# Issuing the small q loads from GpSimd in place of the sync engine, in a fused attention and feed-forward kernel

## The chip, the cores and the metric

The kernel runs on one core of a Trainium2 chip. The metric is the device time of one launch in microseconds (us). Before the change the median of three runs was 926.68 us (926.6 to 928.33). The profiled execution has a span of 926.5 us, at a granted TensorE clock of 1.00.

A core has TensorE (matmul), VectorE, ScalarE and GpSimd, which compute; the sync engine, which only issues transfers; and 16 DMA engines, which carry them. In the profile these are PE (PEld is TensorE's weight load), DVE, ACT, POOL and SP. A name with q behind it, such as SPq, is the engine's instruction queue, which issues transfers and waits for semaphores.

## The reference

```python
q, k, v: (8 batches, 8 heads, 576 rows, 64)      # float32
kv  = einsum('bhsd,bhse->bhde', k, v)            # 64 x 64 per head, no softmax
out = einsum('bhsd,bhde->bhse', q, kv)
out = out / sqrt(mean(out*out, axis=-1) + 1e-6) * g_norm
x   = out.transpose(0, 2, 1, 3).reshape(4608, 512)
h   = x @ w_in                                   # w_in: 512 x 2048
g   = h * erf(softplus(h))
return g @ w_out                                 # w_out: 2048 x 512, result 4608 x 512
```

Linear attention with a normalization per row and head gives x; a feed-forward block with an unusual gate follows.

## The kernel before

**Groups.** The 4608 rows of x are cut into nine groups (`NG`) of 512 rows. Group T takes the first 512 rows of batch T; the ninth gathers the last 64 rows of all eight batches. For a group, the attention is made for four pairs of heads (`NP`), one after the other, while the feed-forward block of the group before is running. So a pair of group T+1 is a guest in the work on group T.

**Stages.** The weights come in as 64-bit words and are turned into float32 on ScalarE and VectorE (`load_w`, `w_split`, `w_join`) while group 0 is computed with plain float32 matmuls. From group 1 on (`T == FIRST - 1`) the work moves to faster products with float32r: every weight block is cut into three parts (`w_upper` on ScalarE, L596; `w_lower` on VectorE, L599 and L602), the parts are written to device memory (stores at L668 and L672), and from group 2 on they are fetched again for each group (`load_parts`, L773). A product (L634) is eight matmuls into `n_ps` and four into `m_ps`. From group 2 on the work goes in batches of four of the sixteen column blocks of w_in (`BATCH`); one batch takes about 24 us, and one pair of heads is a guest in each.

**Loads of a pair.** `load_pair(i)` fetches k and v of pair i with transfers of 288 KB or 287.5 + 0.5 KB (L141, L146). In group 0, q comes in whole (L132) and TensorE turns it. From group 1 on, `load_q` fetches q so that VectorE can turn it with one instruction per pair (L318, the transpose of 32 x 32 blocks): it needs each 32-column piece of a head in a place of its own. So q of a pair is taken in eight transfers of 32 or 40 KB, whose contiguous runs have 32 numbers, 128 bytes (L162).

**Order and queues.** The order of all instructions is written by hand; each engine's queue runs in program order and waits in order. Nearly all transfers are issued by the sync engine: q, k, v, the raw weights, the stores of cut weights, the fetches of weight parts and the results. A transfer that waits, for instance for a free buffer, holds back everything behind it on that queue. The tiles of q have two buffers (`kvp`, `bufs=2`), those of pairs 2 and 3 excepted. From group 1 on, pair i+2 is loaded in the step `loads`, next to the work on pair i; its q takes the buffer that the transpose of pair i has freed. GpSimd issues the two loads of `g_norm` at the start and sets up some constants; nothing stands on its queue afterwards.

**The deferral.** For the first two pairs of group 1 (pairs 4 and 5), `load_pair(..., turned=False)` brings only k and v. Their q is put later into the sync queue by hand: `load_q(NP)` after all raw weight loads of the opening (L758), and `load_q(NP + 1)` in the second step of group 0 (L906).

Of the kernel before, what the change touches and what calls it, by code (L numbers as in the profile page):

```python
# [61 lines left out]
def kernel(  # L62
# [10 lines left out]
    nc = tc.nc  # L73
# [6 lines left out]
    NP = H // 2  # L80
# [38 lines left out]
    def chunks(T):  # L119

        return 6 if T == 0 else 5

    def load_pair(i, turned=True):
        T, p = divmod(i, NP)
        if T >= B:
            return
        pool = early if i in (2, 3) else kvp
        side = nc.scalar if i < 3 else nc.sync
        if T == 0:
            t = pool.tile([P, G if pool is early else S], FP32, name="q_sb", tag="q")  # L130
            t = q_sb[T, p] = t[:, 0:G].rearrange("p (j h d) -> p j h d", j=J, h=2)
            nc.sync.dma_start(  # L132
                out=t, in_=q[T, 2 * p : 2 * p + 2, 0:G, :].rearrange("h (p j) d -> p j h d", j=J)
            )
        for name, got, src in (("k", k_sb, k), ("v", v_sb, v)):
            C = chunks(T)
            rows, rest = divmod(S, C)
            assert rest < 2
            t = got[T, p] = pool.tile([rows + rest, 2, C, D], FP32, name=f"{name}_sb", tag=name)
            heads = src[T, 2 * p : 2 * p + 2]  # L140
            side.dma_start(  # L141
                out=t[:rows].rearrange("r h c d -> r h (c d)"),
                in_=heads[:, : S - rest].rearrange("h (r c) d -> r h (c d)", c=C),
            )
            if rest:
                side.dma_start(  # L146
                    out=t[rows:, :, 0], in_=heads[:, S - rest :].rearrange("h r d -> r h d")
                )
        if T > 0 and turned:
            load_q(i)  # L150

    def load_q(i):


        T, p = divmod(i, NP)
        t = q_sb[T, p] = kvp.tile([P, S], FP32, name="q_sb", tag="q")
        for n in range(P // SQ):
            h, w = divmod(n, D // SQ)
            to = t[n * SQ : n * SQ + SQ].rearrange("a (j b) -> a j b", b=SQ)
            for head, js in ((1 - h, slice(0, G // 2 // SQ)), (h, slice(G // 2 // SQ, S // SQ))):  # L160
                src = q[T, 2 * p + head, :, w * SQ : w * SQ + SQ]
                nc.sync.dma_start(  # L162
                    out=to[:, js], in_=src.rearrange("(j a) b -> a j b", a=SQ)[:, js]
                )

# [108 lines left out]
    def w_next(what):  # L274
        i = w_at[what]
        if i < len(w_order):
            w_at[what] = i + 1
            {"load": load_w, "split": w_split, "join": w_join}[what](*w_order[i][1:])
# [465 lines left out]
    for i in range(NP + 3):  # L744
        for piece, p in ((0, i), (1, i - 1), (4, i - 3), (3, i - 2)):
            if 0 <= p < NP:
                first[p][piece]()
        if i == 1:
            for _ in range(RAW - 2):
                w_next("load")  # L750
            load_pair(NP, turned=False)
            load_pair(NP + 1, turned=False)
        for what in w_rounds.get(i, ()):
            w_next(what)


    w_late.append(True)
    load_q(NP)  # L758
    first_batch, batches = FIRST * NB, NG * NB
    w_seq = {  # L760
        which: [(which, f) for _ in range(NG - FIRST) for f in range(FC)] for which in ("in", "out")
# [60 lines left out]
    for n in range(FIRST * FC + 1):  # L822
        T, f = divmod(n, FC)
        if n == FC:
            early_room.close()
            late = ctx.enter_context(tc.tile_pool(name="late", bufs=1))
            x_new = ctx.enter_context(tc.tile_pool(name="x_new", bufs=1))
            acc = ctx.enter_context(tc.tile_pool(name="acc", bufs=1))
            w_in_p = ctx.enter_context(tc.tile_pool(name="w_in_p", bufs=BATCH))
            low = low_room.enter_context(tc.tile_pool(name="low", bufs=1))  # L830
            forms = late.tile([P, 3, KC, G], FP32R, name="x_forms0")
            x_forms[FIRST] = [forms[:, i] for i in range(3)]
        if T < FIRST:
            if f == 0:
                steps = pieces_of(T + 1)

            if due(0 if n == 2 * (BATCH - 1) else 1):
                weights()
            while kept:
                keep_prepared()  # L840
            for piece in steps[f][3]:
                piece()
            for key in list(w_new)[:2]:
                w_lower(*key)
            for piece in steps[f][0]:
                piece()
        while due(0):
            weights()
        done = n - LAG + 1
        if T == 0 and done >= 0:  # L850
            gates(done)
        if T == FIRST - 1:
            if f == 0:
                x_high = wide.tile([P, KC, G], FP32R, name="x_high", tag="a")
                x_low = low.tile([P, KC, G], FP32R, name="x_low")
                for i in range(0, KC, 2):
                    upper(xT[T][:, i : i + 2], x_high[:, i : i + 2])
                for i in range(0, KC, 2):
                    lower_only(xT[T][:, i : i + 2], x_high[:, i : i + 2], x_low[:, i : i + 2])
        if T == FIRST - 1 and f >= WHOLE:  # L860
            n_ps, m_ps = hidden(T, f, turns=False)
        elif T < FIRST:

            if n > 1:
                plain[n] = ps_h.tile([P, G], FP32, name="h_ps", tag="h")
                blocks = [(n, c) for c in range(KC)]
            elif n == 0:
                for i, (pool, tag) in enumerate(((ps_at, "at"), (ps_o, "o0"))):
                    plain[i] = pool.tile([P, G], FP32, name="h_ps", tag=tag)
                blocks = [(i, c) for c in range(KC - 1) for i in range(2)] + [(0, KC - 1)]  # L870
            else:
                blocks = [(1, KC - 1)]
            for i, c in blocks:
                nc.tensor.matmul(  # L874
                    plain[i],
                    lhsT=w_in_sb[:, i % FC, c],
                    rhs=xT[T][:, c, :],
                    start=(c == 0),
                    stop=(c == KC - 1),
                )  # L880
        if T < FIRST:
            if n == whole:
                old_h = acc.tile([P, BATCH, G], FP32, name="h", tag="e")
            h = hs[n] = old_h[:, n - whole] if n >= whole else unit("h_sb")
            s = ss[n] = unit("s_sb")
            if n in plain:
                nc.scalar.copy(h, plain.pop(n))
            else:
                nc.scalar.activation(h, n_ps, AF.Copy, scale=SHIFT - 1.0)
                add(h, m_ps)  # L890
            if T == FIRST - 1:
                if f == 1:
                    x_both = wide.tile([P, KC, G], FP32R, name="x_both", tag="b")
                    for i in range(0, KC, 2):
                        both_only(x_high[:, i : i + 2], x_low[:, i : i + 2], x_both[:, i : i + 2])
                    x_forms[T] = x_high, x_low, x_both
                gates(done)
                for key in list(w_new):
                    w_lower(*key)
                for key in to_cut[f]:  # L900
                    w_upper(*key)
            nc.scalar.activation(s, h, AF.Softplus)
            if n == 0:
                w_next("split")
            if n == 1:
                load_q(NP + 1)  # L906
            for piece in steps[f][1]:
                piece()
            if f % BATCH == BATCH - 1:
                for i in range(n - BATCH + 1, n + 1):  # L910
                    nc.scalar.activation(ss[i], ss[i], AF.Erf)  # L911
                softplus_table()
            if T == FIRST - 1:
                load_parts("in", {FC - 3: 2, FC - 2: 1, FC - 1: 1}.get(f, 0))
        if n >= LAG:
            T2, f2 = divmod(n - LAG, FC)
            last = n - LAG in (FC - 1, whole - 1)
            project(f2, hs[n - LAG], last)
            if last:
                sums(*((acc, "e") if T2 < FIRST - 1 else (wide, "a")))  # L920
                if T2 == 0:
                    for j in range(J):
                        store(T2, j, es.pop(j))
        if T < FIRST:
            for piece in steps[f][2]:
                piece()
# [49 lines left out]
    for m in range(first_batch, batches + 1):  # L976
        T, b = divmod(m, NB)
# [133 lines left out]
```

## Time and profile before

| Item | Value |
|---|---|
| median time | 926.68 us |
| TensorE busy | 898.8 us, 97% of the span |
| VectorE, ScalarE, GpSimd busy | 751.0, 589.9, 2.4 us |
| bytes moved by DMA | 259.91 MB in 143,210 packets |
| packets under 512 bytes | 78,936 |
| sync engine's queue of transfers (q1) | 141,432 packets, 256.74 MB, 75.7% of 16 engines |
| GpSimd's queue of transfers (q0) | 64 packets |
| q transfers from the sync engine after group 0 | 224 (112 of 40 KB, 112 of 32 KB) |

The busy time of TensorE is modelled, since matmuls overlap, and TensorE at 97% is not TensorE at its peak. The share of a DMA queue is the time that its packets took, out of 16 engines' span. An instruction that issues a transfer is not counted as busy; its duration on the queue is the time until the queue can go on. A wait is put down to the semaphore that came last.

### The profile page before, as it was taken

How to read it: one execution, taken by the hardware profiler on the slowest of the kernel's cores; microseconds unless marked ns; L12 is line 12 of the kernel's file. 1: busy time of each engine (PE TensorE's matmuls, PEld its weight loads, DVE VectorE, ACT ScalarE, POOL GpSimd, SP SyncE). 2: the span in 40 equal slices, each digit the busy share in tenths (PEclk: the TensorE clock that was granted, in tenths of full speed). 3: DMA queues.
4: the chain of work that ended last, by engine and by line, in shares of the span. 5: the costliest groups of instructions: out<-in, count | busy, mean ns of one | idle time of the engine just before them, and what ended most of it. 6: DMA issues, size and time to landing. Idle time of an engine off the chain costs nothing.

```text
span 926.5 us, 13591 instructions
## 1 busy us (share of the span) xinstructions
PE 898.8 (97%) x4990; PEld 668.6 (72%) x4990; DVE 751.0 (81%) x1088; ACT 589.9 (64%) x783; POOL 2.4 (0%) x10
## 2 busy tenths in 40 slices
PE   6999999988999999999999999999999999999998
PEld 4444445655587888778878888788878888888886
DVE  2799958888588888888888888888888888886777
ACT  3868766767675666656665666666666766665552
POOL 1000000000000000000000000000000000000000
PEclk9999999999999999999999999999999999999999
DMA  9767506698688888988898788887889788778871
GB/s 250 237 190 265 167 1 249 246 378 313 239 287 312 311 312 310 347 308 308 308 337 309 296 310 310 301 306 284 292 313 404 272 286 322 291 288 314 325 271 51
DMA packets 143210, 259.91 MB, mean 281 GB/s; under 512 B 78936, under 2 KB 101800, under 8 KB 143144
## 3 DMA queue, kind: packets, MB, share of 16 engines
q1 hardware_dynamic: 141432, 256.74, 75.7%
q10 hardware_dynamic: 1648, 2.29, 0.9%
q8 instruction: 40, 0.66, 0.3%
q14 instruction: 26, 0.21, 0.1%
q0 software_dynamic: 64, 0.00, 0.0%
HBM read 224.40 MB, written 34.60 MB: 280 GB/s over the span
## 4 chain that ended last, share of the span: by engine, by line
PE 76%; DMA 11%; DVE 6%; ACT 5%; issue 1%; SPq 1%; DVEq 0%; ACTq 0%
PE n_ps L634 41%; PE m_ps L634 20%; PE o_ps L690 6%; PE h_ps L874 4%; DMA w_out_parts<-w_out 4%; DMA w_in_parts<-w_in 2%; DMA w_in<-w_new 2%; DMA v_sb<-in_v_dram 1%; PE at_ps L449 1%; PE at_ps L435 1%; DMA w_raw<-in_moe_w_out_dram 1%; ACT s_sb L911 1%; DMA q_sb<-in_q_dram 1%; DVE h L612 1%; PE at_ps L496 1%
## 5 line engine op out<-in xcount | busy, mean ns | idle before, releaser
L634 PE MATMUL n_ps<-w_out_parts,g_forms 128*128 128x512 f32 x928 | 231.2, 391 | 1.7 <-DMA w_out_parts<-w_out 1.7
L634 PE MATMUL n_ps<-x_forms,w_in_parts 128*128 128x512 f32 x896 | 225.1, 393 | 3.2 <-DMA w_in_parts<-w_in 2.1
L634 PEld LDWEIGHTS n_ps<-w_out_parts,g_forms 128*128 128x128 f32 x928 | 172.4, 188 | 38.4 <-DMA w_out_parts<-w_out 3.3
L634 PEld LDWEIGHTS n_ps<-x_forms,w_in_parts 128*128 128x128 f32 x896 | 166.1, 188 | 41.1 <-ACT h L1024 3.2
L1039 ACT ACTIVATE s<-h 128x512 f32<-128x512 f32 x112 | 71.0, 634 | 180.9 <-DVE h L612 180.9
L612 DVE TENSOR_TENSOR h<-m_ps,h 128x512 f32<-128x512 f32 x116 | 79.9, 689 | 61.5 <-ACT h L1024 39.9
L634 PE MATMUL m_ps<-w_out_parts,g_forms 128*128 128x512 f32 (+1 forms) x468 | 124.3, 388 | 0.0
L634 PE MATMUL m_ps<-x_forms,w_in_parts 128*128 128x512 f32 x448 | 119.8, 389 | 0.0
L690 PE MATMUL o_ps<-w_out_sb,h_sb 128*128 128x512 f32 x224 | 101.5, 596 | 0.2 <-DVE h_sb L820 0.2
L634 PEld LDWEIGHTS m_ps<-w_out_parts,g_forms 128*128 128x128 f32 x468 | 87.5, 188 | 18.4
L634 PEld LDWEIGHTS m_ps<-x_forms,w_in_parts 128*128 128x128 f32 x448 | 84.1, 188 | 17.6
L612 DVE TENSOR_TENSOR e<-m_ps,e 128x512 f32<-128x512 f32 (+1 forms) x117 | 80.3, 687 | 14.1 <-PE m_ps L634 2.9
L1024 ACT ACTIVATE h<-n_ps 128x512 f32<-128x512 f32 x112 | 65.6, 585 | 16.6 <-PE n_ps L634 16.6
L690 PEld LDWEIGHTS o_ps<-w_out_sb,h_sb 128*128 128x128 f32 x224 | 41.3, 189 | 45.3 <-issue 42.8
L578 DVE SCALAR_TENSOR_TENSOR g_forms<-g_forms 128x1024 fp32r<-128x1024 f32 x58 | 71.1, 1225 | 2.0
L575 DVE TENSOR_TENSOR g_forms<-h,g_forms 128x1024 fp32r<-128x1024 f32 x58 | 70.6, 1217 | 1.2 <-ACT g_forms L572 1.1
L572 ACT ACTIVATE g_forms<-h 128x1024 fp32r<-128x1024 f32 x58 | 58.7, 1051 | 14.8 <-PE m_ps L634 10.9
L1071 DVE TENSOR_TENSOR h<-h,s 128x1024 f32<-128x1024 f32 x56 | 65.9, 1218 | 0.0
L874 PE MATMUL h_ps<-xT,w_in_sb 128*128 128x512 f32 x144 | 64.6, 594 | 0.0
L607 DVE SCALAR_TENSOR_TENSOR e<-n_ps,e 128x512 f32<-128x512 f32 x88 | 60.1, 683 | 1.5 <-PE n_ps L634 1.5
L109 ACT ACT_TABLE_LOAD x44 | 56.5, 1283 | 0.8
L874 PEld LDWEIGHTS h_ps<-xT,w_in_sb 128*128 128x128 f32 x144 | 27.1, 190 | 33.4 <-issue 31.6
(119 smaller groups left out, 990.7 us busy)
## 6 DMA issues: line engine op xcount, KB each, us to landing
w_out_parts<-w_out SPq DMA_DIRECT2D x116, 768.0 KB
w_in_parts<-w_in SPq DMA_DIRECT2D x112, 768.0 KB
w_in<-w_new SPq DMA_DIRECT2D x16, 768.0 KB
w_raw<-in_moe_w_in_dram SPq DMA_DIRECT2D x16, 512.0 KB
w_raw<-in_moe_w_out_dram SPq DMA_DIRECT2D x8, 1024.0 KB
out_dram<-e SPq DMA_DIRECT2D x32, 256.0 KB
k_sb<-in_k_dram SPq DMA_DIRECT2D x28, 287.5 KB
v_sb<-in_v_dram SPq DMA_DIRECT2D x28, 287.5 KB
```

Source lines behind the costliest of these rows:

```text
L109: nc.scalar.preload_act_table_set("softplus")
L572: nc.scalar.activation(high, x, AF.Copy, scale=1.0 + 2.0**-13)
L575: nc.vector.tensor_tensor(out=low, in0=x, in1=high.bitcast(FP32), op=ALU.subtract)
L578: nc.vector.scalar_tensor_tensor(out=both, in0=low.bitcast(FP32), scalar=SHIFT, in1=high.bitcast(FP32), op0=ALU.mult, op1=ALU.add,)
L607: nc.vector.scalar_tensor_tensor(out=out_, in0=ps, scalar=scale, in1=out_, op0=ALU.mult, op1=ALU.add)
L612: nc.vector.tensor_tensor(out=out_, in0=ps, in1=out_, op=ALU.add)
L634: nc.tensor.matmul(ps[:, cols], lhsT=weights(form, k), rhs=moving(form, k)[:, cols], start=(form == forms[0] and k == 0), stop=(form == fo ...
L690: nc.tensor.matmul(o_ps[j], lhsT=g[:, j * P : j * P + P], rhs=w_out_sb[:, f, :], start=(f == 0), stop=last,)
L874: nc.tensor.matmul(plain[i], lhsT=w_in_sb[:, i % FC, c], rhs=xT[T][:, c, :], start=(c == 0), stop=(c == KC - 1),)
L1024: nc.scalar.activation(h[:, i], n_ps, AF.Copy, scale=SHIFT - 1.0)
L1039: nc.scalar.activation(s[:, i], h[:, i], AF.Softplus)
L1071: nc.vector.tensor_tensor(out=part(h, half), in0=part(h, half), in1=part(s, half), op=ALU.mult)
```

## The change

From group 1 on, the eight transfers of q per pair are issued by GpSimd, whose queue is empty by then, and no longer by the sync engine. The runs, the buffers and the bytes are the same. With q on a queue of its own, the deferral is taken out as well: `load_pair` issues q of pairs 4 and 5 with their k and v, and the two separate calls of `load_q` go. The purpose is to keep the many small issues out of the queue that carries the weights.

```diff
-    def load_pair(i, turned=True):
+    def load_pair(i):
...
-        if T > 0 and turned:
+        if T > 0:
             load_q(i)
...
                 src = q[T, 2 * p + head, :, w * SQ : w * SQ + SQ]
-                nc.sync.dma_start(
+                nc.gpsimd.dma_start(
                     out=to[:, js], in_=src.rearrange("(j a) b -> a j b", a=SQ)[:, js]
                 )
...
-            load_pair(NP, turned=False)
-            load_pair(NP + 1, turned=False)
+            load_pair(NP)
+            load_pair(NP + 1)
...
     w_late.append(True)
-    load_q(NP)
...
-            if n == 1:
-                load_q(NP + 1)
```

## The prediction, made before the changed kernel was run

> **What bounds the kernel now.** I first read the page: busy shares, then the slices.
>
> ```profile
> PE 898.8 (97%) x4990; PEld 668.6 (72%) x4990; DVE 751.0 (81%) x1088; ACT 589.9 (64%) x783; POOL 2.4 (0%) x10
> ...
> DMA  9767506698688888988898788887889788778871
> ```
>
> TensorE is the bound, GpSimd is empty, and the DMA engines are some 80% busy without being full. Only TensorE's 27.7 us of idle time (926.5 - 898.8) can be won, and only where it goes back to the sync queue. A table by stretch places it: 8.6 us in the first 24 us, 2.6 in 24 to 48, 3.4 in 192 to 216, 2.8 in 216 to 240, 4.1 spread over 336 to 720, and 4.0 at the very end. The list of waits names the ends of these:
>
> ```profile
> DVE qT L318 <- DMA q_sb<-in_q_dram: 3.9, 1, 3.9
> PE n_ps L634 <- DMA w_in_parts<-w_in: 2.1, 2, 1.7
> PE at_ps L435 <- DVE qT L318: 2.0, 1, 2.0
> PE n_ps L634 <- DMA w_out_parts<-w_out: 1.7, 2, 0.9
> ```
>
> Columns: total us, times, longest. The two waits on weight parts (2.1 + 1.7 = 3.8 us) are nearly all of the 4.1 us. Then the sync queue's timeline before the longest:
>
> ```profile
> 581.89 7.43 SPq L162 DMA_DIRECT2D q_sb<-in_q_dram  x8
> 589.37 0.46 SPq L773 DMA_DIRECT2D w_out_parts<-w_out  x1
> 589.92 0.38 SPq L773 DMA_DIRECT2D w_in_parts<-w_in  x1
> 590.34 0.43 SPq L773 DMA_DIRECT2D w_out_parts<-w_out  x1
> 590.87 0.75 SPq L773 DMA_DIRECT2D w_in_parts<-w_in  x1
> ```
>
> Eight q transfers keep the sync queue for 7.43 us; then weight loads go out one after the other without a wait, so their buffers had been free and the loads were late only because q stood in front. In the chain, the last of these (issued 590.87) lands 10.12 us later and TensorE waits 1.7 us for it. The other three stalls show the same picture: q blocks of 7.83, 10.71 and 11.30 us end at 369.9, 466.5 and 661.3, and weights issued some us later arrive 0.8, 0.9 and 0.4 us late. While q is issued from 581 to 590 the DMA share is 0.55, against 0.82 around it: the queue is short of issue, not of bandwidth.
>
> Stage two (144 to 250 us) shows the same for stores:
>
> ```profile
> 177.41 7.30 SPq L162 DMA_DIRECT2D q_sb<-in_q_dram  x8
> 184.82 0.39 SPq L672 DMA_DIRECT2D w_out<-w_new  x1
> ...
> 188.13 0.63 ACT L596 ACTIVATE w_new<-w_out_sb 128x512 fp32r<-128x512 f32 x1 [1.44 <-DMA w_out<-w_new]
> 190.12 0.63 ACT L596 ACTIVATE w_new<-w_in_sb 128x512 fp32r<-128x512 f32 x1 [1.36 <-DMA w_in<-w_new]
> ...
> 197.25 0.49 PE L634 MATMUL n_ps<-x_high,w_new 128*128 128x512 f32 x1 [3.42 <-ACT h_sb L889]
> ```
>
> q delays the store of a cut weight, the store frees its buffer late, ScalarE waits 2.8 us, and TensorE waits for ScalarE.
>
> **What the Trainium skill says.** "DMA: Bandwidth & Descriptors", section "Issuing engines are not separate DMA queues": all issuers feed the same 16 engines, and another issuer saves only the sequencer's issue time. The issue time is just what is short here. Its section "SWDGE vs HWDGE vs iDMA" says that GpSimd's cores compute each descriptor in software, and that each DMA engine goes round its queues in turn. This trace has only two GpSimd transfers:
>
> ```profile
> L174 POOL DMA_DIRECT2D g_col<-in_g_norm_dram x2: 531/618/704, 1.2 to 1.9; - x2
> ```
>
> Each has 64 runs of one number, so this is a weak gauge. "SBUF — State Buffer", section "Who interferes with whom": VectorE's copies and tensor_scalar in a two-port mode and GpSimd exclude each other. The trace has such candidates: the CAST at L480 takes 426 ns for 512 columns, where L481 takes 692.
>
> **The change part by part.**
>
> Sync queue, removed: 28 pairs x 8 issues. A block lasts about 7.4 us without back pressure and up to 14.77 us for two pairs at the start; 28 x 7.5 = 210 us of the queue's time go. Its other work moves up only where it was ready.
> - Steady stage: the late weights were 0.4 to 1.7 us late after q blocks of at least 7.4 us. Even with q's data still sharing the engines, they come in time. Gain 3.8 us.
> - Stage two: ScalarE's 1.44 + 1.36 us before the erf batch vanish, as the stores can go about 5 us earlier. TensorE's stall of 3.42 us shrinks by 2.8. The stall at 227 us stays: there ScalarE's last wait before the erf batch is for TensorE itself (1.31 us at 220.0), so its DMA wait of 2.15 us at 218.05 gains nothing. Gain 2.8 us.
> - Start: q of the first pair of group two is issued at 36.51, behind weights, and lands at 47.64. VectorE waits 3.9 us, TensorE 2.0. From GpSimd it starts when TensorE has turned pair 0 (9.9 us) and lands by about 31 us. Gain 2.0 us.
>
> GpSimd, added: 224 transfers. A pair is 576 rows x 2 heads x 2 halves = 2304 runs of 128 bytes, 256 or 320 per transfer. Unknown: the cost of a descriptor. Lower bound, all of the 0.62 us is fixed: 5 us per pair. Upper bound, all of it is per descriptor: 0.62/64 x 2304 = 22.3 us. I take 1.5 us a transfer, 12 us per pair. Nothing else is queued on GpSimd, the transposes of successive pairs (L318) are 24.2 us apart, and a q buffer freed by one transpose is read two transposes, 48 us, later. Even 22.3 us is hidden. Cost 0.
>
> DMA engines: the q runs are small. After q has ended, 768 to 816 us, 310 GB/s take a share of 0.79: 48 x 16 x 0.79 / 14.88 MB = 40.8 engine-us per MB. Queue 1 in all: 0.757 x 16 x 926.5 = 11,222 engine-us against 256.74 x 40.8 = 10,475. The 747 over, shared by 64,512 q packets, are 11.6 ns each on top of 5.2 for the bytes: 16.8 ns, or 2.4 us of all engines per pair. Unchanged if software descriptors are as cheap. To fill the 18% left free in a period of 24.2 us (4.4 us), a packet would have to cost (4.4 + 2.4) x 16 / 2304 = 47 ns.
>
> VectorE lock: the next pair's CAST and small copies come 20 us after the transpose that releases q, so 12 us of descriptor writing misses them. In stages one and two, tensor_scalar (L250, L253) can collide, but from 50 to 190 us TensorE has no idle time at all, so what feeds it has slack, and VectorE is idle 11 us in 120 to 144. Bound 0 to 3 us; I take 0.
>
> Start, moved: the deferral goes too, so q of pairs 4 and 5 competes from 10 us on with k and v of pair 3 (issued 11.2 and 14.1, read at 20.29 without a wait) at a DMA share of 0.91. Bound: 0 if there is slack, 4.8 us if both pairs (2 x 2.4) go first. GpSimd's pace lets about one through, half of it into slack: 1.2 us lost.
>
> Sum: 926.7 - 3.8 - 2.8 - 2.0 + 1.2 = 919.3 us.
>
> **The rivals.**
> - Larger gain: no loss at the start, and earlier stores and weights also take in 4 us of what is not counted above, ScalarE's other waits on stores (9.3 - 2.8 = 6.5 us) and TensorE's weight loads on the DMA (3.3): 926.7 - 8.6 - 4 = 914 us. Against it: most of these waits lie beside others.
> - A wash: the start loses 4.8 us and VectorE's lock 3, so 926.7 - 8.6 + 7.8 = 926 us. For it: the share of 0.91 there.
> - Slower, the packets: a software-made q packet costs 60 ns. Then q takes 8.6 us of all engines per pair, the need exceeds the period by 8.6 - 2.4 - 4.4 = 1.8 us, and over some 15 steady pairs less the 4.8 us of gains at the start and in stage two: 926.7 + 27 - 4.8 = 949 us; half of it if prefetched weights cushion it, 935. Against it: no view of before shows such a price.
> - Slower, the generator: 3.5 us per transfer make 28 us per pair, 4 us over the period, over 24 pairs near 1010 us. The gauge above (at most 2.8 us for an average transfer) speaks against it.
>
> **How the numbers follow.** Forecast (gain of 4 to 10 us) 60%, larger gain 8%, wash 13%, packets 13%, generator 6%. Predicted 919.3. The range from 914.5 to 935 leaves out the generator, the worse packets and the largest gain. Faster 0.68, same 0.12, slower 0.20.
>
> **What would show it.** Right: no wait of TensorE for weight parts; the transpose L318 at about 44 us without a DMA wait; ScalarE's waits for stores shorter between 184 and 192; GpSimd's eight issues inside 24 us per pair. Wrong: a wait of L318 for q in every pair (generator), a DMA share near 1.0 with new weight stalls (packets), TensorE waiting for k or v at 20 us (start), longer CASTs (lock). The prediction falls with the descriptor's price above all.

## The result: 936.6 us, 1.2% slower

The changed kernel took 936.59 us (median of four, 935.79 to 941.56), the kernel before beside it 926.64 us (925.43 to 928.33). The ratio is 1.0117, 95% interval 1.0078 to 1.0156. The forecast was 919.3 us, faster; the time lies just outside the range.

Busy time and DMA slices of the changed kernel, from the page:

```profile
PE 904.2 (97%) x4990; PEld 668.4 (71%) x4990; DVE 752.0 (80%) x1088; ACT 589.6 (63%) x783; POOL 135.5 (14%) x234
...
DMA  9867406888799898889797889888797788778871
```

GpSimd now has 135.5 us of work, of which the issues of q are 133.1 (on GpSimd the page counts them as busy). The matmuls are the same 4990; TensorE's busy time is 5.4 us longer, but the ends of matmuls are modelled, so nothing is read into it. TensorE's waits for weight parts became (total us, times, longest)

```profile
PE n_ps L634 <- DMA w_in_parts<-w_in: 10.7, 14, 2.5
PEld n_ps L634 <- DMA w_out_parts<-w_out: 6.1, 9, 1.2
PE n_ps L634 <- DMA w_out_parts<-w_out: 2.4, 4, 0.8
```

The two PE lines were 3.8 us together; they are 13.1 us, and come 18 times, not four. (The middle line, of TensorE's weight load, was 3.3 us, five times.) The changed kernel was not behind everywhere. At 144 us the two were level; in stage two the changed kernel won, and at 244 us it was 4.0 us ahead. The matmul that had waited 3.42 us at 197.25 waits 0.87, and the second stall of that stage, at 227.12, has shrunk too (its line before, then both after):

```profile
227.12 0.50 PE L634 MATMUL n_ps<-x_high,w_new 128*128 128x512 f32 x1 [2.79 <-ACT h L889]
...
194.78 0.50 PE L634 MATMUL n_ps<-x_high,w_new 128*128 128x512 f32 x1 [0.87 <-ACT h_sb L888]
223.09 0.50 PE L634 MATMUL n_ps<-x_high,w_new 128*128 128x512 f32 x1 [1.21 <-ACT h L888]
```

From 244 us to the end it lost 12.8 us: TensorE's idle time from 288 to 720 us is 432 - 186.32 - 232.10 = 13.6 us where it was 4.1. So the loss is in the steady stage, where the forecast had put its largest gain.

GpSimd's transfers, from the view of the tile q_sb, and the two queues of the page:

```profile
L162 POOL DMA_DIRECT2D q_sb<-in_q_dram x224: 584/601/1128, 9.9 to 662.4; - x112
DMA to landing us min/median/max: 1.9/5.7/10.0
```

```profile
q1 hardware_dynamic: 73336, 248.47, 73.1%
q0 software_dynamic: 7232, 8.27, 3.8%
```

An issue takes 601 ns in the median, eight of them under 5 us a pair. The 64,512 packets of 128 bytes have become 3,584 of 2,048 or 2,560 bytes; q takes 3.8% of 16 engines, 569 engine-us, or 8.8 ns per run. Neither the making of the transfers on GpSimd nor their packets are dear.

Now the sync queue around one pair, start and duration, changed kernel first:

```profile
500.89 0.29 SPq L141 DMA_DIRECT2D k_sb<-in_k_dram  x1
...
504.55 1.13 SPq L141 DMA_DIRECT2D v_sb<-in_v_dram  x1
506.38 0.56 SPq L146 DMA_DIRECT2D v_sb<-in_v_dram  x1
508.38 6.54 SPq L772 DMA_DIRECT2D w_out_parts<-w_out  x1
515.01 0.37 SPq L772 DMA_DIRECT2D w_in_parts<-w_in  x1
```

```profile
503.81 0.56 SPq L146 DMA_DIRECT2D v_sb<-in_v_dram  x1
505.68 11.26 SPq L162 DMA_DIRECT2D q_sb<-in_q_dram  x8
516.99 0.45 SPq L773 DMA_DIRECT2D w_out_parts<-w_out  x1
517.55 0.37 SPq L773 DMA_DIRECT2D w_in_parts<-w_in  x1
```

The second fence is the kernel before. Without q, the first weight load behind k and v is itself held for 6.54 us. The queue is through with it at 514.92; before, it was through with q at 516.94. Taking q off freed 2 us, not 11: so it was not q alone that had held the q issues. The packets of the trace show what else the engines were doing. Mean number of packets in flight by kind, in steps of 2 us:

```
             before                      after
us       weights  k,v    q        weights  k,v    q
506-508    16.2   0.0  0.0            6.3  2.3  0.0
508-510    12.1   0.5  0.0            1.2  4.2  0.6
510-512     0.7   4.9  2.3            1.0  3.7  3.1
512-514     0.0   5.3  2.4            1.0  0.4  4.4
514-516     0.0   2.0  5.5            2.6  0.1  0.8
516-518     0.0   0.0  4.0           14.2  0.9  0.2
518-520    12.9   0.0  0.0           15.2  1.1  0.0
520-522    15.9   0.0  0.0           15.2  1.1  0.0
```

With weights 16 packets are in flight, with k and v five. The cause is the shape: from group 1 on k and v come as 115 rows of five, and 115 = 5 x 23. The Trainium skill, "DMA: Bandwidth & Descriptors", section "Why a DMA increments its semaphore by 16 and not by 1", says that a transfer runs on the largest number of engines up to 16 that divides the slowest dimension of both sides. For 115 that is five; the trace agrees with 4.9 to 5.3 in flight. So it was in the forecast's stretch with a DMA share of 0.55: from 584 to 586 us 5.3 k or v packets, 1.7 of q and 0.2 of weights were in flight. What the forecast read as a queue short of issue was five engines at work on k and v, and the other eleven with only some small q packets.

An estimate of what these five carry per batch, from median packet times: weights 64 x 234 ns = 15.0 us, k and v 92 x 55 = 5.1, q 144 x 12.5 = 1.8, results 8 x 84 = 0.7: 22.6 us in a period of some 24. The other eleven carry 17.5. The mean share of 0.82 hid this. After the change, q takes 8 packets of 138 ns in the mean of the two sizes, 1.1 us in place of 1.8, so by the same estimate the five carry 21.9 us: the loss isn't that they have more to carry.

And one thing differs after: from 508 to 512 one weight packet is in flight while some four k or v packets are, and from 516 to 522 some fifteen weights and one k or v. From 508.30 to 515.70 us the 22 weight packets follow one another, each starting within about 0.1 us of the end of the one before, and from 515.80 to 522.73 so do 92 k and v packets, just one engine's share of a pair. So one of the five engines still carried weights while its four fellows did k and v, and did its k and v while all others carried weights. A weight load spread over all 16 engines isn't complete before this one has carried its part. Before, q in the middle let all come out level: of the k and v packets between 300 and 660 us, a share of .007 started while 12 or more weight packets were in flight; after, .229. I call this the overlap share.

### The profile page after: what moved, and what is told of

Read it like the earlier page. It is cut to its first block, busy times and chain, and to the rows that moved or that the text cites. A ratio compares the mean times of both kernels' runs of the same rounds, so it can differ in the third digit from the quotient of the medians.

```text
span 935.3 us, 13621 instructions
## 1 busy us (share of the span) xinstructions
PE 904.2 (97%) x4990; PEld 668.4 (71%) x4990; DVE 752.0 (80%) x1088; ACT 589.6 (63%) x783; POOL 135.5 (14%) x234
## 4 chain that ended last, share of the span: by engine, by line
PE 57%; DMA 29%; DVE 6%; ACT 5%; issue 2%; SPq 0%; DVEq 0%; ACTq 0%
PE n_ps L634 29%; PE m_ps L634 14%; DMA w_out_parts<-w_out 14%; DMA w_in_parts<-w_in 8%; PE h_ps L873 6%; PE o_ps L690 5%; DMA k_sb<-in_k_dram 4%; DMA w_in<-w_new 2%; DMA q_last<-in_q_dram 1%; DVE w_new L599 1%; DMA q_sb<-in_q_dram 1%; PE at_ps L449 1%; ACT s_sb L908 1%; DVE h L612 1%; PE at_ps L435 1%
## 5 line engine op out<-in xcount | busy, mean ns | idle before, releaser
L162 POOL DMA_DIRECT2D q_sb<-in_q_dram x224 | 133.1, 602 | 522.7 <-DVE qT L318 514.9
```

The lines of the kernel that those rows point to most:

```text
L162: nc.gpsimd.dma_start(out=to[:, js], in_=src.rearrange("(j a) b -> a j b", a=SQ)[:, js])
```

## The experiments

**Theory:** k and v on five engines, nearly full, are the limit; weights directly behind k and v let one of them fall behind. **Rivals:** GpSimd's packets among the weights; the deferral; the one-row transfers. (That GpSimd issues q too late is out already: after, L318 never waits for q.) Each ratio is to the kernel before, run on the same chip in turn.

**1 and 2. Even engines.** k and v as 128 rows of four and 64 of one (both multiples of 16), once on the changed kernel, once on the kernel before. It also saves 112 small matmuls in all (4878 for 4990); the trace shows 38 of their kind in 0.75 us, so that they are worth some 2 us at most.

```diff
+            if T > 0:
+                rows, rest, C = P, R, J
...
-                out=t[:rows].rearrange("r h c d -> r h (c d)"),
+                out=t[:, :, 0:C].rearrange("r h c d -> r h (c d)"),
...
-                    out=t[rows:, :, 0], in_=heads[:, S - rest :].rearrange("h r d -> r h d")
+                    out=t[:rest, :, C], in_=heads[:, S - rest :].rearrange("h r d -> r h d")
```

> The changed kernel, with k and v of groups 1 to 7 fetched as 128 rows of 4 x 64 plus 64 rows of 64 in place of 115 rows of 5 x 64 plus one row (18 small matmuls a pair in place of 20). Theory A (uneven engines: k and v of 115 rows are carried by five of the sixteen DMA engines, one of the five falls behind once q no longer stands between k, v and the weights, and each weight load ends with it): the waits for weight parts vanish, about 916 to 921 us, and no slower than the kernel before with the same edit. Theory B (the GpSimd queue itself slows the weight loads, whatever k and v do): weight waits stay, 928 to 936 us, and clearly slower than the kernel before with the same edit.

> The kernel before (q on the sync engine, deferral kept) with the same even split of k and v. Theory A: its four stalls for weights behind q shrink too, since the q issues are no longer held up by five full engines: 918 to 924 us, near a_even. Theory B: 918 to 924 us as well, but a_even 1% above it.

Measured: 919.55 us, ratio 0.9915 (0.9901 to 0.9928), and 919.18 us, ratio 0.9911 (0.9897 to 0.9924). TensorE waits for no weight part in either. The stretch from 480 to 528 us of the changed kernel and then of its even version (TensorE, its weight load, VectorE, ScalarE, GpSimd, clock, DMA share, GB/s):

```profile
480.00:528.00 48.00, 45.42 (x275) 36.11 (x278) 40.31 (x59) 28.91 (x37) 9.36 (x16) 1.00 0.84 296
```

```profile
480.00:528.00 48.00, 47.40 (x296) 38.56 (x295) 40.85 (x61) 30.08 (x41) 8.87 (x17) 1.00 0.92 330
```

In this stretch the share and the rate rise, since k and v no longer leave eleven engines idle; from 300 to 660 us the difference is smaller (0.85 to 0.87, 302 to 307 GB/s). The sync queue of the even version waits for TensorE to free buffers for 367.6 us, where that of the changed kernel did for 199.2, so it is further ahead:

```profile
SPq L773 <- PE m_ps L635: 367.6, 109, 11.4
```

With even engines the two kernels differ by 0.4 us, so it makes no difference who issues q. That the change loses needs the uneven load.

**3. Another issuer than GpSimd:** ScalarE, `nc.scalar.dma_start` at L162.

> The changed kernel with q's eight issues on ScalarE's queue in place of GpSimd's: again a queue of its own, but with descriptors made in hardware. Theory A: one engine falls behind just the same, weight waits of 10 us or more, and ScalarE loses issue time besides: 935 to 950 us. Theory B (software descriptors are what hurts): no weight waits beyond those of before, 920 to 930 us, unless ScalarE's own issue time shows as waits of TensorE for ScalarE.

Measured: 1124.35 us, ratio 1.2107 (1.2078 to 1.2137). ScalarE's own instructions stand behind its issues, and TensorE behind these:

```profile
ACT h L1021 <- DMA q_sb<-in_q_dram: 147.5, 16, 12.2
PE n_ps L634 <- ACT h L1021: 96.6, 18, 8.4
```

Both expectations miss by far: the kernel is so much slower (DMA share 0.70 from 300 to 660 us, granted clock 0.922 over the span) that weights are never short, and for its question the run says nothing. It shows that issues can hold up a computing engine for 12 us.

**4. GpSimd alone, deferral kept** (the kernel before with `nc.gpsimd` at L162).

> The kernel before with GpSimd as issuer and the deferral kept: the change without its second part. Theories A and B: the loss lies in the steady stage, so 934 to 938 us, like the changed kernel. Theory C (the loss comes from q of pairs 4 and 5 competing at the start): near 925 us.

Measured: 937.56 us, ratio 1.0111 (1.0089 to 1.0133), overlap share .327. The issuer alone makes the whole loss.

**5. The deferral alone** (the changed kernel with `nc.sync` at L162).

> The changed kernel with the sync engine as issuer again: the second part of the change alone (q of pairs 4 and 5 asked for early, no deferral). All theories put the loss in the steady stage, so this gives 924 to 932 us; theory C (the loss comes from the start) would give 936.

Measured: 932.62 us, ratio 1.0036 (1.0021 to 1.0051), overlap share .007. This is just above the expectation. Dropping the deferral costs something with the sync engine as issuer, but does not add to the loss with GpSimd (1.0111 without, 1.0117 with it).

**6. Weights directly behind k and v, without GpSimd:** in the kernel before, `load_q(i)` stands ahead of k and v from pair 6 on.

> The kernel before, q still on the sync engine with hardware descriptors, but from pair 6 on the eight q transfers are issued ahead of the pair's k and v in place of behind them, so that weights follow directly on k and v. Theory A (what hurts is that nothing stands between the uneven k, v and the weights): one engine falls behind as in the changed kernel, waits for weight parts of 8 us or more, 932 to 940 us, with GpSimd out of the picture. Theory B (GpSimd's queue is needed for the loss): 924 to 929 us.

Measured: 951.31 us, ratio 1.0240 (1.0202 to 1.0278), overlap share .089, slower than either expectation.

```profile
PE n_ps L634 <- DMA w_in_parts<-w_in: 17.7, 20, 1.9
```

The order loses without any q transfer of GpSimd, but by a different route: q's issues hold the queue for 12 to 14 us there, and all five engines come late to the weights, not one. So the run shows a loss without GpSimd, and doesn't test the single late engine.

**7. A brake in place of q:** in the changed kernel, a store of 256 bytes of the v tile on the sync queue behind each pair's k and v from pair 8 on. The store must wait for v, so the weights do too.

```diff
+        if T > 1:
+            nc.sync.dma_start(out=dram.tile([1, D], FP32, name=f"brake{i}"), in_=t[0:1, 0, 0])
         if T > 0:
             load_q(i)
```

> The changed kernel with one more transfer on the sync queue behind each pair's k and v from pair 8 on: 256 bytes of the v tile to a scratch in device memory. It makes the sync queue wait until v has landed on all five engines before weights go out. Theory A: the lagging engine is waited for once per pair, so it cannot stay behind; the share of k and v packets that run beside weights on twelve or more engines falls from 24% to some 2%, and the time to 922 to 929 us. Theory B: weights go out later still and the slow queue stays, 937 us or more.

Measured: 927.37 us, ratio 0.9992 (0.9974 to 1.0009), overlap share .007.

```profile
PE n_ps L636 <- DMA w_in_parts<-w_in: 3.0, 1, 3.0
```

GpSimd issues the same 224 transfers, and the 13.1 us of TensorE's waits for weight parts shrink to one of 3.0. So the loss comes with the missing step between k, v and weights. The time doesn't reach the forecast 919; by the sum above (software q at 1.1 us in place of 1.8) the five engines still carry 21.9 us per batch.

**8. Without the one-row transfers** of k and v (L146), from group 1 on. The last row of each head's k and v is left out in these groups.

> The changed kernel without the one-row transfers of k and v from group 1 on; it leaves out the last row of every head's k and v in those groups. The five-engine loads of 115 rows stay. Theory A: the load on five engines is what counts, so still 932 to 938 us with weight waits. Rival: the one-row transfers, which held the sync queue for up to 4.6 us, were what the even split really removed; then 918 to 924 us.

Measured: 938.56 us, ratio 1.0100 (1.0060 to 1.0141), overlap share .283. The one-row transfers do not make the late engine late.

**9. GpSimd's packets added, q left where it was:** the kernel before plus 208 GpSimd transfers of 288 runs of 128 bytes into a spare tile that nothing reads, eight behind each transpose (L318).

> The kernel before, with its q loads left on the sync queue, plus eight further GpSimd transfers per pair (288 runs of 128 bytes each, 2304 per pair as q has) into a spare tile that nothing reads, released by the transpose as q's are in the changed kernel. It adds work and leaves out none. If order is the cause (q no longer stands between k, v and the weights): the DMA engines stay in step, the share of k and v packets that run beside weights on 12 or more engines stays under 0.05, and the time is 926 to 931 us, the extra bytes costing 1.2 us of 23.8 on each engine per pair. If the software queue's traffic by itself makes one engine fall behind: that share goes to 0.2 or more, and the time to 935 us or above.

Measured: 987.27 us, ratio 1.0617 (1.0574 to 1.066), overlap share .003.

```profile
PE n_ps L647 <- DMA w_in_parts<-w_in: 30.4, 29, 3.2
```

The order theory was right on the share and wrong on the time by 56 us; the rival the other way round. So software packets among the others do not put an engine out of step while q stands between, but 1.0 us more per engine and batch (eight packets of 129 ns) brings the estimate for the five to 22.6 + 1.0 = 23.6 us of 24. That alone doesn't yet exceed the period, but it counts median packets: in the mean, a k or v packet takes 68 ns here and 56 before. A part may not be the DMA's: TensorE's granted clock is 0.986 over the span.

**10. The even kernel with GpSimd as issuer and the deferral kept.**

> The kernel before with k and v cut into 128 rows of four and 64 of one, q issued by GpSimd, and the deferral of the first two q loads kept. If an even load of the DMA engines leaves nothing for q's place to win, it takes 918.5 to 920 us, as the two even kernels measured so far. If removing the deferral cost the even version of the changed kernel the 3 us that it cost on the sync queue, and the moved issue won them back, it takes 916 us.

Measured: 919.66 us, ratio 0.9895 (0.9864 to 0.9926). The three even kernels lie within 0.5 us, so neither issuer nor deferral matters there. No version here beats 919.2 us.

**11. The extra transfers of run 9 on the even kernel** of run 2.

> The evenly cut version of the kernel before (919.2 us), with the same 208 extra GpSimd transfers into a spare tile that made the uneven kernel 987 us. It adds work and leaves out none. If five nearly full engines are what the extra traffic ran into: here each engine has several us of room per pair, 1.1 us more of packets fit, and the time is 919 to 924 us, with next to no wait of TensorE for weight parts. If GpSimd's traffic slows the kernel by itself, by its packets' place among the weights or by the clock: 940 us or more here as well.

Measured: 932.73 us, ratio 1.0040 (1.0026 to 1.0055). Between the two expectations. Weight waits stay small:

```profile
PE n_ps L648 <- DMA w_out_parts<-w_out: 2.1, 3, 0.9
PE n_ps L648 <- DMA w_in_parts<-w_in: 1.9, 4, 0.8
```

The same traffic costs 58 us with uneven engines and 13.5 us with even ones. So most of run 9's loss needs the uneven load. The 13.5 us are not all explained: the DMA share is 0.96 to 0.98 from 288 to 720 us, and TensorE loses 2.6 us of busy time in 144 to 288 us.

**12. No q at all from group 2 on:** the changed kernel reads group 1's two q tiles again, so the q of later groups is left out.

> The changed kernel without any load of q from group 2 on: the two q tiles of group 1 are read again, so the q of the later groups is left out. Weights stand directly behind k and v on the sync queue, and there is neither q nor GpSimd traffic beside them. If the order alone makes one of the five engines fall behind: the share of k and v packets that run beside weights on 12 or more engines stays at 0.1 or more, with TensorE waits for weight parts of some us in all, and 925 to 935 us. If it takes q packets among the weights: that share is under 0.05, no waits for weight parts, and 917 to 921 us.

Measured: 919.71 us, ratio 0.9902 (0.9880 to 0.9924), no wait of TensorE for weight parts, overlap share .169. Again each expectation is half right. The order alone, without one q packet, does let k and v run beside weights. But here all five engines do it together (5.0 to 5.4 k and v packets beside 11 weights at 500 to 504 us), no engine is left alone, and each has the 1.1 us per batch more (eight packets of 138 ns) that q had taken. So the overlap by itself is harmless. That it costs when one engine is behind and has no time left to catch up is how I read this run beside the others; no run shows it directly.

## Why the prediction was wrong, point by point

- **What bounds (failed).** "While q is issued from 581 to 590 the DMA share is 0.55, against 0.82 around it: the queue is short of issue, not of bandwidth." The low share was that of five engines at work on k and v, and the long q blocks stood behind this backlog: without q, the first weights behind k and v were through the queue 2 us earlier, not 11 (506 to 518 us above).
- **Sync queue, "28 x 7.5 = 210 us of the queue's time go" (failed).** They went from L162, and most came back at L772: its issues take 165.4 us in all where they took 96.3 (as L773), and it has new waits for k and v (total us, times, longest):

```profile
SPq L772 <- DMA k_sb<-in_k_dram: 50.2, 13, 4.6
SPq L772 <- DMA v_sb<-in_v_dram: 32.2, 13, 4.3
```

- **Steady stage, "Even with q's data still sharing the engines, they come in time. Gain 3.8 us" (failed; this is the step that turned the sign).** TensorE's waits for weight parts were to vanish; they grew from 3.8 to 13.1 us, and from 244 us on there is a loss of 12.8 us. The forecast counted q only as a delay in front of the weights. It was also the step that brought the 16 engines back in line (run 7: put a step back, and the waits go), on engines with little room (runs 1, 2, 9, 12: take load off the five or add to it, and the time follows).
- **Stage two, gain 2.8 us (mechanism right, size too small).** The first stall shrank by 2.55 us, near the forecast 2.8. The second, at 227 us, was to stay; it shrank too, from 2.79 to 1.21 us, and the kernel was 4.0 us ahead.
- **Start, gain 2.0 less 1.2 (the sum was too good by 0.8).** L318 starts at 45.55 without the DMA wait, 2.2 us earlier; but the products of the opening begin 1.7 us later (30.10, before 28.39), at a DMA share of 1.00 in the first 24 us where it was 0.91, and at 57.8 us the kernels are level.
- **Generator, 12 us per pair (hidden as said, size off).** It takes 4.8 us, near the lower bound of 5: GpSimd waits 514.9 us for the transposes, and L318 never waits for q.
- **VectorE's lock, 0 (right in size).** The CAST takes 426 ns in both, but only one of its 31 ran beside a GpSimd issue, so it tests little. L253, of which seven of 18 did, takes 644 ns, before 634 (means over its two forms): 0.2 us in all.
- **The rival "packets"** named a time near the result for the wrong reason: a run costs 8.8 ns, not 60 (and before, where the forecast reckoned 16.8 ns, a q packet took 12.5). Its sum of needs against the period was the right kind of sum, but over 16 engines in place of the five.

**Open.** Why just one of the five falls behind, and which: the packets of the trace don't name their engine. The one-row transfers are excluded (run 8), and GpSimd's packets alone do not do it while q stays between (run 9). Without q packets none stays alone behind (run 12), so it seems to take both the order and q among the weights, but no run shows the mechanism.

## What to carry to other kernels

Before a low DMA share is read as missing issue, count the packets in flight: a row count whose largest divisor up to 16 is small, as 115 with five, puts a transfer on a few engines, and the sum to hold against the period is that of the fullest engine. A transfer on an in-order queue is also a step between its neighbours; when it moves elsewhere, ask what now stands next to what. And cure the uneven load first: here it gave 0.9%, after which it made no difference who issues q.

## What was not expected of the hardware

- Runs of 128 bytes issued by GpSimd are recorded 16 or 20 to a packet of 2,048 or 2,560 bytes (121 and 155 ns in the median); issued by the sync engine each is its own packet of 12.5 ns in the mean, so 16 take 200 ns.
- An issue can hold its queue for microseconds while transfers ahead of it are still under way: 6.54 us for the weight load at 508.38 us with k and v on five engines, 13.84 us for eight q loads (run 6), and on ScalarE's queue also the computing behind it (run 3).
- The granted TensorE clock was 0.986 over the span of run 9 and 0.93 in its stretch from 480 to 528 us, though TensorE had the same matmuls; with the same transfers on even engines (run 11) it was 0.999. Why is open.
